# An FFT-filter and GELU-MLP kernel: the order of the first loads, the slots of batch 1's transform, and the slots of GpSimd's tables

## The chip, the cores and the metric

One core of one Trainium2 chip. The metric is the device time of one execution, in microseconds. The kernel takes x and the weights in float32 and gives float32; inside it works in bf16 and fp16.

Times in the text are microseconds from the start of the profiled span. A "slot" is one step of the main loop, defined below.

## The reference

```python
# x: (8, 3008, 256); filt_r, filt_i: (1505, 256); w_in: (256, 2048); w_out: (2048, 256)
X = np.fft.rfft(x, axis=1)
Y = X * (filt_r + 1j * filt_i)[None]
y = np.fft.irfft(Y, n=3008, axis=1).reshape(24064, 256)
h = y @ w_in
g = 0.5 * h * (1 + erf(h / sqrt(2)))
out = g @ w_out
```

So each of 8 batches goes through a global filter along its 3008 rows, and all 24064 rows go through a two-layer MLP with an exact GELU.

## The kernel before

**The transform.** The Fourier transform of length 3008 = 47 x 64 is done as small matmuls in four steps, s1 to s4. s1 is a transform over 47 rows; its result goes to DRAM (R1, stores on SP's queue) and comes back with other rows on the partitions (r1, tile b_sb). s2 is the transform over 64 with the twiddles; VectorE multiplies its result by the filters (s2_out, four products per unit) and adds the pairs (s2_sum, two pairs per unit). s3 is the first step back; ScalarE evicts it (s3_out), it goes to DRAM (R2) and comes back (r2, tile d_sb). s4 gives y, in a ring in SBUF. s1 works in four pieces c = 0 to 3 of the batch's input, s2 and s3 in three units u = 0 to 2, s4 in eight groups of two halves. Ahead of s1, fold takes sum and difference of the two halves of the input rows, on VectorE. Batch 0 has its own, quicker path (c1 to c4), which runs before the main loop.

**The MLP.** The rows are taken in 47 tiles of 512. mm1 makes 128 hidden columns of a tile (two matmuls of 512 columns, then a GELU on ScalarE); a tile takes 16 of them. mm2 multiplies by w_out. Tiles 0 and 2 do it plainly (mm2_first, 64 matmuls of 256 columns); all others with seven products in place of eight (mm2_seven, 112 matmuls of 128 columns), for which VectorE makes sums and differences of the hidden values (sums_1, four per tile; sums_2 and sums_3, two each) and of w_out (weight_sums, once).

**The main loop** counts slots s. Slot s does, in this order: what was put at s in a table written by hand (fold, s1, r1, s2, ..., tables), the share of the last tile's mm2, and one mm1 of tile s // 16. Every engine runs its instructions in the order in which this loop writes them. The mm2 of tile 0 begins at slot 10, four matmuls a slot to slot 15, and 8 for each 3 slots after that. Tile 5 is the first that needs batch 1's y: in its first six slots (80 to 85) no mm1 is done, and s4 of batch 1 begins at slot 82.

**Banks.** PSUM has three pools in the loop: "h" with 3 banks (mm1; one is lent to s1 with c > 1, to s2 and to s3), "o" with 2 banks (mm2; one is lent to s1 of batch 1 with c < 2, line 428), and "f" with 3 banks (s1 to s4, tables). An s1 takes four banks: VectorE evicts two of them, the lent one first, ScalarE the two others (lines 435 to 438).

**GpSimd.** GpSimd issues the loads that change the type (x, w_in, w_out; load_x_pairs and load_w_out), the later stores of the output (put_rows), and makes the tables: T1g and T2g (table_4_rows), wt (weights_4), pick (table_u_pick), T2p (table_2_parities), and T4a in four parts of eight columns w each (table_4_all, lines 406 to 416: two fp32 products and a sum, twice). It also loads half the rearranged filters (load_filters_again). s2 needs T2p and the filters, s3 needs U (table_u: two matmuls with pick), s4 needs T4a, each part for two groups. gate(t) (line 143) copies one element of t on GpSimd, so that what follows in GpSimd's queue starts only when t has been written.

**The first loads.** Ahead of the loop GpSimd issues batch 1's input, c = 0 then c = 2 (each call brings two pieces: c and c + 1), 12 transfers in all, and then the two halves of w_out:

```python
897    for c in (0, 2):
898        for h in range(2):
899            m.load_x_pairs(1, c, h, 2)
900    m.load_w_out(0)
901    m.load_w_out(8)
```

**Places of batch 1 before.** fold at slots 0, 1, 5, 8; s1 at 4, 7, 10, 12; r1 at 16; s2 at 30, 43, 56; s3 11 slots after each s2, at 41, 54, 67; r2 of piece 0 at 71. T1g, T2g, wt, pick and T2p are put at slot 0, table_4_factors at 14, table_u at 18, T4a's parts at 15, 45, 52 and 104.

Of the kernel before, what the change touches and what calls it, by code (L numbers as in the profile page):

```python
# [31 lines left out]
class _Mix:  # L32
# [385 lines left out]
    def s1(self, b, c):  # L418

        nc = self.nc  # L420
        if c == 0:
            self.st[b, "R1"] = self.dram.tile([NB, 48, 256], BF16, tag="R1", name="R1")
        if b == 1 and c == 3:
            at = self.pp.tile([128, 2, 4, 256], BF16, tag="p12", name="p12").rearrange("p t k c -> p (t k) c")
        else:
            at = self.pa.tile([128, 8, 256], BF16, tag="a", name="a_sb")
        x = self.st[b, "s", c], self.st["x1"][:, 1, 4 * c:4 * c + 4]
        lent = "o" if b == 1 and c < 2 else "h"
        ps = [[self.bank("ps_s1", lent if i == v == 0 else "f") for v in range(2)] for i in range(2)]
        for i in range(2):  # L430
            for d in range(2):
                for v in range(2):
                    nc.tensor.matmul(ps[i][v][64 * d:64 * d + 64, :], lhsT=self.T1s[64 * v:64 * v + NA],  # L433
                                     rhs=x[d][64 * v:64 * v + NA, 2 * i:2 * i + 2, :], start=True, stop=True)
        for i in range(2):
            for v in range(2):
                w = 4 * v + 2 * i
                self._evac(at[:, w:w + 2, :].rearrange("p w c -> p (w c)"), ps[i][v], "act" if v else False)
        for d in range(2):
            for v in range(2):  # L440
                w = HB * d + 16 * v + 4 * c
                nc.sync.dma_start(out=self.st[b, "R1"].rearrange("n q c -> q n c")[:, w:w + 4],
                                  in_=at[64 * d:64 * d + 48, 4 * v:4 * v + 4])
# [344 lines left out]
def kernel(  # L788
# [9 lines left out]
    m = _Mix(ctx, tc, x, filt_r, filt_i, moe_w_in, moe_w_out, out)  # L798
    nc, B, S = tc.nc, m.B, m.S
# [3 lines left out]
    g = m.small  # L803
    wide = ctx.enter_context(ExitStack())
    m.psum(wide, w=(2, 1), m=(1, 1), n=(5, 1))
    act = "act"
# [90 lines left out]
    for c in (0, 2):  # L897
        for h in range(2):
            m.load_x_pairs(1, c, h, 2)
    m.load_w_out(0)  # L900
    m.load_w_out(8)

    warm = g.tile([128, 1], FP32, name="warm")
    nc.scalar.activation(out=warm, in_=m.p, func=AF.Gelu)
# [9 lines left out]
    at = {}  # L914

    def put(slot, f, *a):
        at.setdefault(slot, []).append((f, a))

    def first(b):
        return (b * S // TCH) * 16  # L920

    busy, crowd, after = set(), set(), {}
    for b in range(1, B):
        hi = first(b)
        e = 4 * (b == B - 1)
        s1, n1, r1 = (4, 2.75, 16) if b == 1 else (hi - 87, 3.7, hi - 73) if b == 2 else (hi - 94 - e, 3.7, hi - 80 - e)
        s2 = (30, 43, 56) if b == 1 else (hi - 74, hi - 59, hi - 44) if e else (hi - 64 + (b == 2), hi - 48, hi - 32)
        busy.update(range(s1 - 1, s1 + int(3 * n1) + 2))
        for c in range(4):
            slot = s1 + int(c * n1 + (b == 1 and c in (1, 2)))  # L930
            put((0, 1, 5, 8)[c] if b == 1 else (70, 74, 86, 94)[c] if b == 2 else hi - 94 - (20, 13, 8, 6)[c], m.fold, b, c)
            put(slot, m.s1, b, c)
        for u in range(3):
            put(r1 if u < 2 else s2[0] + 1, m.r1, b, u)
            put(s2[u], m.s2, b, u)
            for i in range(4):
                put(s2[u] + 2 * i + (b == 2 and u == 0), m.s2_out, b, u, i // 2, i % 2)
            for i in range(2):
                put(s2[u] + (9 + i if 1 < b < B - 1 else 7 + 2 * i), m.s2_sum, b, 2 * u + i)
            s3 = s2[u] + (11 if b == 1 else 12 if e or (b, u) in ((2, 0), (B - 2, 2)) else 13)  # L940
            put(s3, m.s3, b, u)
            put(s3 + 1, m.s3_out, b, u, 1)
            busy.update(range(s2[u] - 1, s2[u] + 5), range(s3 - 1, s3 + 2))
        after[b] = s3 + 4
        crowd.update(range(s2[0], after[b]), range(s1 + 66, s1 + 94))
        if b + 1 < B:
            for i, (u, o, p) in enumerate(((0, 5, 1), (0, 7, 1), (1, 1, 2), (1, 5, 3), (1, 7, 3), (2, 1, 4), (2, 5, 5), (2, 7, 5))):
                put((76, 77, 80, 81)[i - 4] if b == 1 and i > 3 else s2[u] + o, m.load_next, b, p, i // 2, i % 2)

    for b in range(1, B):  # L950
        end = 1000000
        if b == B - 1:
            s4 = first(b) - 17
            for u in range(16):
                put(s4 + u, m.s4, b, u // 2, u % 2, act if u % 2 else False)
            for c in range(4):
                put(after[b] if c < 3 else s4 + 5, m.r2, b, c)
            continue
        for u in range(7, -1, -1):
            due = (b * S + GRP * u) // TCH * 16  # L960
            end = min(end, due - 2 if u or b > 1 else 83)
            if b == u == 1:
                end = 85
            for half in (1, 0):
                while end in busy:
                    end -= 1
                assert end > after[b] + 7
                put(end, m.s4, b, u, half, act if half or end in crowd or b == 1 and u == 0 else False)
                busy.add(end)
                end -= 1 if u < 3 else 2  # L970
            if u % 2 == 0:
                put(after[b] if u == 0 else end - 11, m.r2, b, u // 2)

    put(0, m.table_4_rows, g)
    put(0, m.weights_4, g)
    put(0, m.table_u_pick, g)
    put(0, m.table_2_parities)
    put(14, m.table_4_factors, g)
    put(18, m.table_u)
    parts = [(w, h) for w in range(0, HB, 8) for h in range(2)]  # L980
    for i, slot in enumerate((15, 45, 52, 104)):
        put(slot, m.table_4_all, parts[2 * i:2 * i + 2])
    put(1, m.load_filters_again, nc.gpsimd, 0, 2)
    put(18, m.load_filters_again, nc.sync, 2, 4)
    put(20, m.weight_sums)
    plain = (0, 2)
# [55 lines left out]
```

## Time and profile before

| | us |
|---|---|
| median of 3 runs | 737.6 (737.28 to 738.28) |
| the profiled execution, time | 737.13 |
| its span | 735.3 |
| first GELU of the main loop | 38.9 |
| ScalarE: 752 GELUs of 0.603 | 445.7 busy |
| VectorE: 84 filter products of 1.217 | 101.9 busy |
| GpSimd: issue of output stores | 131.7 busy |

The span is shorter than the device time by what lies around it, 1.8 us here. Busy TensorE counts pipelined matmuls with modelled ends, so a short stand between two matmuls hardly shows in the total: it is seen in the timeline of TensorE, where an instruction's idle time ahead of it and what released it stand in brackets. DVE is VectorE, ACT ScalarE, POOL GpSimd, SP the engine that issues most transfers between SBUF and DRAM.

In this execution the granted TensorE clock is 1.00 in all stretches of the span.

### The profile page before, as it was taken

The numbers are of one execution on the slowest core, as the hardware profiler recorded it, in microseconds if no ns is written. First come the engines' busy times: TensorE is split into PE (matmuls) and PEld (weight loads), VectorE is DVE, ScalarE is ACT, GpSimd is POOL, SyncE is SP. The second block draws the span as 40 slices with busy tenths as digits, with TensorE's granted clock in tenths as the row PEclk, the third lists the DMA queues.
The fourth block names the chain that finished last, engine by engine and source line by source line (L and its number), as shares of the span: only waits on it lengthen the run. The fifth ranks groups of instructions, "written<-read, shape, count | busy, mean of one in ns | idle before, by whom it ended". The sixth has DMA issues, their size and how long they took to land.

```text
span 735.3 us, 22145 instructions
## 1 busy us (share of the span) xinstructions
PE 716.1 (97%) x9063; PEld 506.5 (69%) x9213; DVE 604.6 (82%) x1105; ACT 575.4 (78%) x1049; POOL 291.2 (40%) x547
## 2 busy tenths in 40 slices
PE   8999999999999999999999999999999999999998
PEld 4856666677777767676677767666677767777776
DVE  8886797899887998789986989779998898675566
ACT  6997677688887888778887788877888788777773
POOL 7895744656122553134621355114631122122121
PEclk9999999999999999999999999999999999999999
DMA  8996435655345643545545455455544433311011
GB/s 145 211 187 213 107 91 116 196 144 110 83 132 172 125 99 105 149 145 117 119 124 171 104 115 124 116 151 132 120 109 127 148 100 102 111 38 52 30 58 59
DMA packets 81190, 89.30 MB, mean 121 GB/s; under 512 B 13201, under 2 KB 60433, under 8 KB 81089
## 3 DMA queue, kind: packets, MB, share of 16 engines
q0 software_dynamic: 22480, 40.02, 23.8%
q1 hardware_dynamic: 58193, 47.66, 23.4%
q8 instruction: 72, 1.18, 0.7%
q14 instruction: 29, 0.24, 0.1%
q10 hardware_dynamic: 416, 0.20, 0.1%
HBM read 55.57 MB, written 48.23 MB: 141 GB/s over the span
## 4 chain that ended last, share of the span: by engine, by line
PE 88%; DVE 3%; DMA 3%; POOL 2%; issue 2%; ACT 1%; DVEq 0%; POOLq 0%
PE ps_o L719 40%; PE ps_h L643 38%; PE ps_s L518 3%; DMA x_sb<-in_x_dram 2%; PE ps_o L659 2%; PE ps_s L433 2%; PE ps_s L491 2%; PE ps_s L460 2%; DMA F<-in_filt_i_dram 1%; ACT g_sb L646 1%; DVE g_sb L694 1%; POOL F L141 1%; DVE s_sb L688 1%; DVE a_sb L331 1%; POOL x_sb L90 0%
## 5 line engine op out<-in xcount | busy, mean ns | idle before, releaser
L646 ACT ACTIVATE g_sb<-ps_h 128x512 f16<-128x512 f32 x752 | 445.7, 603 | 138.8 <-PE ps_h L643 114.9
L643 PE MATMUL ps_h<-y_sb,w_in_sb 128*128 128x512 bf16 (+3 forms) x1454 | 414.2, 365 | 0.6
L766 POOL DMA_DIRECT2D out_dram<-ost x231 | 131.7, 577 | 380.5 <-DVE ost L748 370.0
L719 PEld LDWEIGHTS <-g_sb 128*128 128x128 f16 x2880 | 188.9, 98 | 84.4 <-issue 14.4
L719 PEld LDWEIGHTS <-s_sb 128*128 128x128 f16 x2160 | 145.3, 98 | 53.4 <-issue 3.1
L643 PEld LDWEIGHTS <-w_in_sb 128*128 128x128 bf16 x1600 | 125.7, 98 | 7.6 <-issue 1.3
L719 PE MATMUL ps_o<-w_sums,g_sb 128*128 128x128 f16 x1440 | 124.9, 219 | 2.4 <-DVE g_sb L694 0.9
L719 PE MATMUL ps_o<-w_sums,s_sb 128*128 128x128 f16 x1440 | 123.3, 219 | 1.9 <-DVE t_sb L734 0.2
L688 DVE TENSOR_TENSOR s_sb<-g_sb 128x1024 f16<-128x1024 f16 x180 | 119.2, 693 | 0.7 <-ACT g_sb L646 0.6
L719 PE MATMUL ps_o<-w_out_sb,g_sb 128*128 128x128 f16 x1440 | 116.4, 219 | 1.8
L471 DVE TENSOR_TENSOR p<-ps_s,F 128x1024 bf16<-128x1024 f32 x84 | 101.9, 1217 | 9.4 <-PE ps_s L460 8.0
L99 POOL DMA_DIRECT2D x_sb<-in_x_dram x156 | 79.4, 516 | 2.8 <-DMA x_sb<-in_x_dram 1.0
L694 DVE TENSOR_TENSOR g_sb<-s_sb,g_sb 128x1024 f16<-128x1024 f16 x90 | 63.7, 708 | 1.5
L719 PE MATMUL ps_o<-w_out_sb,s_sb 128*128 128x128 f16 x720 | 62.5, 219 | 0.9
L701 DVE TENSOR_TENSOR s_sb<-g_sb 128x1024 f16<-128x1024 f16 x90 | 61.5, 684 | 0.0
L741 DVE TENSOR_TENSOR t_sb<-t_sb,ps_o 128x256 f32<-128x256 f32 x45 | 18.8, 417 | 39.8 <-PE ps_o L719 39.3
L518 PEld LDWEIGHTS <-d_sb 96*128 96x128 bf16 x448 | 31.3, 97 | 26.0 <-issue 1.3
L329 ACT ACTIVATE y_sb<-ps_s 128x376 bf16<-128x376 f32 x95 | 45.5, 479 | 3.1 <-PE ps_s L518 3.1
L329 ACT ACTIVATE v_sb<-ps_s 128x512 bf16<-128x512 f32 x83 | 45.5, 608 | 1.5 <-PE ps_s L491 1.3
L748 DVE TENSOR_TENSOR ost<-t_sb,ps_o 128x256 f32<-128x256 f32 x88 | 32.9, 415 | 13.9 <-PE ps_o L719 13.8
L331 DVE CAST a_sb<-ps_s 128x512 bf16<-128x512 f32 x54 | 34.7, 684 | 11.6 <-PE ps_s L433 11.4
L736 DVE TENSOR_TENSOR ost<-t_sb,ps_o 128x256 f32<-128x256 f32 x45 | 18.6, 414 | 25.8 <-PE ps_o L719 25.8
(157 smaller groups left out, 563.5 us busy)
## 6 DMA issues: line engine op xcount, KB each, us to landing
out_dram<-ost POOLq DMA_DIRECT2D x127, 128.0 KB, 2.7
b_sb<-R SPq DMA_DIRECT2D x21, 512.0 KB, 4.6
R<-v_sb SPq DMA_DIRECT2D x84, 128.0 KB, 2.4
d_sb<-R SPq DMA_DIRECT2D x56, 192.0 KB, 4.1
R<-a_sb SPq DMA_DIRECT2D x108, 96.0 KB, 2.2
x_sb<-in_x_dram POOLq DMA_DIRECT2D x48, 94.0 KB, 2.8
x_sb<-in_x_dram POOLq DMA_DIRECT2D x48, 48.0 KB, 2.7
x_sb<-in_x_dram POOLq DMA_DIRECT2D x12, 188.0 KB, 5.3
```

Of the source, the lines that this page charges most:

```text
L99: self.nc.gpsimd.dma_start(out=xt[64 * v + to:64 * v + to + m, h, 4 * c:4 * c + 4 * n, :], in_=xv[h][at:at + m, w:w + 4 * n, :])
L329: self.nc.scalar.activation(out=out, in_=in_, func=AF.Copy, scale=1.0 if scale is None else scale)
L331: self.nc.vector.tensor_copy(out=out, in_=in_)
L471: v(out=w[:, a], in0=ps.unsqueeze(2).to_broadcast([128, 2, 2, 256]), in1=f.unsqueeze(1).to_broadcast([128, 2, 2, 256]), op=ALU.mult)
L518: nc.tensor.matmul(ps[:, 94 * i:94 * i + 94], lhsT=d[:, (grp % 2) * 4 + i, 128 * half:128 * half + 128], rhs=self.T4a[:, 4 * grp + i, 0:2 ...
L643: nc.tensor.matmul(ps[:, o:o + n], lhsT=w[:, dc], rhs=self.ring[:, dc, off:off + n], start=(dc == 0), stop=(dc == 1))
L646: nc.scalar.activation(out=self.st["g", t][:, jc, :], in_=ps, func=AF.Gelu)
L688: self.nc.vector.tensor_tensor(out=self.st["s", t][:, i:i + 2], in0=a, in1=b, op=ALU.subtract)
L694: self.nc.vector.tensor_tensor(out=a21[:, k], in0=self.st["s", t][:, k, 0], in1=a22[:, k], op=ALU.add)
L701: self.nc.vector.tensor_tensor(out=self.st["s4", t][:, k], in0=a12[:, k], in1=s2[:, k], op=ALU.subtract)
L719: nc.tensor.matmul(ps[:, (m + 1) % 2, sub, :], lhsT=a[:, i, 128 * sub:128 * sub + 128], rhs=b[:, i], start=i == 0, stop=i == 7)
L766: eng.dma_start(out=out, in_=tile_[lo - r0:lo - r0 + n])
```

## The change

Three things are changed, all near the start of the main loop. The first half of w_out is loaded between the two halves of batch 1's input. Batch 1's transform is put at other slots: s1 at 4, 8, 12, 14, fold at 0, 1, 7, 10, r1 at 18, s2 at 31, 45, 59, and so s3 at 42, 56, 70 and r2 of piece 0 at 74 (s4 stays at 82). GpSimd's tables move: a gate on what fold(1, 3) writes is put at slot 11, and T2p, the filters, pick, T1g, T2g and wt follow it; table_u goes from slot 18 to 24, table_4_factors from 14 to 38; T4a's parts go to 47, 54, 101 and 114, with a gate at 101 on the last a tile of batch 2's s1. In the changed kernel the lines from 427 up to the first loads have a number larger by one.

```diff
--- before.py
+++ after.py
@@ -424,6 +424,7 @@
             at = self.pp.tile([128, 2, 4, 256], BF16, tag="p12", name="p12").rearrange("p t k c -> p (t k) c")
         else:
             at = self.pa.tile([128, 8, 256], BF16, tag="a", name="a_sb")
+        self.st[b, "a"] = at
         x = self.st[b, "s", c], self.st["x1"][:, 1, 4 * c:4 * c + 4]
         lent = "o" if b == 1 and c < 2 else "h"
         ps = [[self.bank("ps_s1", lent if i == v == 0 else "f") for v in range(2)] for i in range(2)]
@@ -897,8 +898,7 @@
     for c in (0, 2):
         for h in range(2):
             m.load_x_pairs(1, c, h, 2)
-    m.load_w_out(0)
-    m.load_w_out(8)
+        m.load_w_out(4 * c)
 
     warm = g.tile([128, 1], FP32, name="warm")
     nc.scalar.activation(out=warm, in_=m.p, func=AF.Gelu)
@@ -923,12 +923,12 @@
     for b in range(1, B):
         hi = first(b)
         e = 4 * (b == B - 1)
-        s1, n1, r1 = (4, 2.75, 16) if b == 1 else (hi - 87, 3.7, hi - 73) if b == 2 else (hi - 94 - e, 3.7, hi - 80 - e)
-        s2 = (30, 43, 56) if b == 1 else (hi - 74, hi - 59, hi - 44) if e else (hi - 64 + (b == 2), hi - 48, hi - 32)
+        s1, n1, r1 = (4, 3.4, 18) if b == 1 else (hi - 87, 3.7, hi - 73) if b == 2 else (hi - 94 - e, 3.7, hi - 80 - e)
+        s2 = (31, 45, 59) if b == 1 else (hi - 74, hi - 59, hi - 44) if e else (hi - 64 + (b == 2), hi - 48, hi - 32)
         busy.update(range(s1 - 1, s1 + int(3 * n1) + 2))
         for c in range(4):
-            slot = s1 + int(c * n1 + (b == 1 and c in (1, 2)))
-            put((0, 1, 5, 8)[c] if b == 1 else (70, 74, 86, 94)[c] if b == 2 else hi - 94 - (20, 13, 8, 6)[c], m.fold, b, c)
+            slot = (4, 8, 12, 14)[c] if b == 1 else s1 + int(c * n1)
+            put((0, 1, 7, 10)[c] if b == 1 else (70, 74, 86, 94)[c] if b == 2 else hi - 94 - (20, 13, 8, 6)[c], m.fold, b, c)
             put(slot, m.s1, b, c)
         for u in range(3):
             put(r1 if u < 2 else s2[0] + 1, m.r1, b, u)
@@ -965,22 +965,24 @@
                 while end in busy:
                     end -= 1
                 assert end > after[b] + 7
-                put(end, m.s4, b, u, half, act if half or end in crowd or b == 1 and u == 0 else False)
+                put(end, m.s4, b, u, half, act if half or end in crowd or b == 1 and u < 2 else False)
                 busy.add(end)
                 end -= 1 if u < 3 else 2
             if u % 2 == 0:
                 put(after[b] if u == 0 else end - 11, m.r2, b, u // 2)
 
-    put(0, m.table_4_rows, g)
-    put(0, m.weights_4, g)
-    put(0, m.table_u_pick, g)
-    put(0, m.table_2_parities)
-    put(14, m.table_4_factors, g)
-    put(18, m.table_u)
+    put(11, lambda: m.gate(m.st["x1"][0:1, 1, 15, 0:1]))
+    put(11, m.table_2_parities)
+    put(11, m.load_filters_again, nc.gpsimd, 0, 2)
+    put(11, m.table_u_pick, g)
+    put(11, m.table_4_rows, g)
+    put(11, m.weights_4, g)
+    put(24, m.table_u)
+    put(38, m.table_4_factors, g)
+    put(101, lambda: m.gate(m.st[2, "a"][0:1, 3, 0:1]))
     parts = [(w, h) for w in range(0, HB, 8) for h in range(2)]
-    for i, slot in enumerate((15, 45, 52, 104)):
+    for i, slot in enumerate((47, 54, 101, 114)):
         put(slot, m.table_4_all, parts[2 * i:2 * i + 2])
-    put(1, m.load_filters_again, nc.gpsimd, 0, 2)
     put(18, m.load_filters_again, nc.sync, 2, 4)
     put(20, m.weight_sums)
     plain = (0, 2)
```

## The prediction

> **What bounds the kernel now.** I read the page's busy shares and its chain first, then busy time by stretch, then the timelines of TensorE, VectorE, GpSimd where the stretches show a hole.
>
> ```profile
> PE 716.1 (97%) x9063; PEld 506.5 (69%) x9213; DVE 604.6 (82%) x1105; ACT 575.4 (78%) x1049; POOL 291.2 (40%) x547
> PE 88%; DVE 3%; DMA 3%; POOL 2%; issue 2%; ACT 1%; DVEq 0%; POOLq 0%
> ```
>
> TensorE is busy 97% of the span and holds 88% of the chain. All matmul work stays after the change, so time moves only by the microseconds in which TensorE stands. Busy time by stretch (us; then PE, PEld, DVE, ACT, POOL) shows where it stands now:
>
> ```profile
> 42.00:46.00 4.00, 3.23 (x24) 1.13 (x22) 3.55 (x7) 4.00 (x9) 3.50 (x15) 1.00 1.22 192
> 70.00:75.00 5.00, 3.87 (x64) 2.39 (x63) 4.74 (x10) 2.72 (x5) 3.39 (x8) 1.00 0.49 71
> 130.00:140.00 10.00, 9.17 (x102) 6.06 (x102) 8.26 (x14) 6.93 (x13) 7.55 (x8) 1.00 0.62 161
> ```
>
> At 42 ScalarE is full (one gelu per slot, plus the evictions of s1); at 70 VectorE is full; at 130 it is slowed. The stalls by name, from the timeline of TensorE:
>
> ```profile
> 73.89 0.65 PE L491 MATMUL ps_s<-p,U 32*64 32x256 bf16 x16 [0.87 <-DVE p L477]
> 77.17 0.41 PE L460 MATMUL ps_s<-b_sb,T2p 64*32 64x256 bf16 x15 [0.22 <-ACT v_sb L329]
> 133.34 0.51 PE L719 MATMUL ps_o<-w_sums,g_sb 128*128 128x128 f16 x6 [0.72 <-DVE g_sb L694]
> ```
>
> And what feeds them, from the timelines of VectorE and GpSimd:
>
> ```profile
> 37.95 1.54 POOL L164 DMA_DIRECT2D w_out_sb<-in_moe_w_out_dram  x2 [0.39 <-DMA x_sb<-in_x_dram]
> 43.27 0.69 DVE L107 TENSOR_TENSOR x_sb<-x_sb 111x1024 bf16<-111x1024 bf16 x1 [0.42 <-DVE a_sb L331]
> 44.60 1.28 DVE L331 CAST a_sb<-ps_s 128x512 bf16<-128x512 f32 x2
> 93.30 2.54 DVE L688 TENSOR_TENSOR s_sb<-g_sb 128x1024 f16<-128x1024 f16 x2
> 130.67 2.62 DVE L694 TENSOR_TENSOR g_sb<-s_sb,g_sb 128x1024 f16<-128x1024 f16 x1
> 131.11 1.61 POOL L414 TENSOR_TENSOR tmp_sb<-t_sb 96x376 f32<-96x376 f32 x2
> ```
>
> The fold at 43.27 is put down to a cast that ended at 42.85; what it truly waits for is the last piece of batch 1's input, whose landing the trace records at 43.09. The two halves of w_out land next, at 46.02 and 49.14: GpSimd's queue lands strictly in order of issue and is never empty from 31 to 49 us. And an f16 add on VectorE, 0.68 alone, took 2.62 and 1.27 while GpSimd's fp32 products (L414, L416) ran.
>
> **The change, part by part** (like for like: TensorE's delay with the same work done).
>
> *A. w_out's first half ahead of input c=2, s1 at slots 4, 8, 12, 14.* The bytes up to and with the input's end are then those that before ended with w_out's first half: the last input lands at 46.02, not 43.09 (+2.9). On VectorE fold(1,2) stands at slot 7, ahead of the casts of s1(1) at slot 8, so these wait too: the first ends 2.15 after the landing (45.24 − 43.09 before), at 48.2. Behind it is TensorE: for c<2 s1 borrows an "o" bank, and the second matmul of mm2 at slot 10 needs that bank. TensorE gets there at about 44.4 (before, gelus 4 to 6 start at 41.82 to 42.78; one s1 less is ahead) and stands until 48.25, 3.8 us. From there: 3 mm2 0.33, mm1 0.43, slot 11 0.87, s1(2) 0.56 (119.36 to 119.92), slots 12 and 13 1.75, s1(3) 0.56: slot 14 at 52.75. Before, slot 14 with all four s1 done began at 50.64. **+2.1**; bounds 1.6 and 2.6, for a landing half a microsecond off. If the input were not delayed, the same count from 45.3 gives 49.8, −0.85.
>
> The longest stand of TensorE now, once the loop runs, is the 0.87 above, and the granted clock is 1.00 in every stretch, so no row prices what 3.8 us of idleness do to the clock; I take nothing for it. The Trainium skill (TensorE: Matmul & The Clock Gate, Part 1) says that an idle window of about 3.4 us halves the clock until about as long a busy one has passed. By that rule a drop would, as an estimate, add 1.7 us to the sum, and this wait would be long enough only by a little.
>
> *B. GpSimd's tables after a gate on fold(1,3).* Before, they filled 39.5 to 54 beside the folds. Now the gate opens 4.12 after the landing (47.21 − 43.09), at 50.1. Behind it in GpSimd's queue: gate 0.4, the T2p copies (eight; 0.49 alone, 5.6 in all as they ran), four F loads 2.25, pick (1.7 from its undisturbed rows, 2.5 as it ran): ready at 58.4 to 60.9. table_u on TensorE moves to slot 24, reached at 52.75 + 7.2 (gelu 14 at 52.00 to gelu 24 at 59.43, less table_u's own 0.24) = 59.95. I take **0**, since VectorE's sums now end before pick begins; bound +0.9. T1g, T2g and the weights (39.54 to 45.73 before) end by 67, ahead of table_4_factors at slot 38. The second w_out half is needed at slot 14, lands at 49. On SP, the last s1 stores go out 2.9 later, so b_sb lands near 62.4, and s2(0) at slot 31 starts near 65.3: hidden, with 2.9 to spare.
>
> *C. s2(0) at 31, s3(0) at 42.* VectorE's queue from s2 to the last sum: four products 1.13, two subtractions and two additions of tile 1 2.5, t 0.35, two L701 1.2, four sums 1.36, L736 and L739 0.78: 10.1, against 10.8 measured before (63.38 to 74.18; the copy of ost, 0.6, now comes ahead of s2). TensorE's own work up to s3 is 9.0 with the factors (0.3), now inside it; 8.6 before. Idle 0.85 in place of 1.7: **−0.85** (0 to −1.2).
>
> *D. s2(1) two slots after s3_out(1), not one.* ScalarE's four v evictions end 2.5 after s3; TensorE now comes 3 × 0.82 = 2.5 after it. The 1.28 that s2(1) took (76.23 to 77.51) falls to 0.6: **−0.65** (0 to −0.7).
>
> *E. T4a's last two parts.* The part that ran at 131 is now gated on the last s1 of batch 2, behind the L694 that it slowed: the 0.72 and its tail go, **−0.8** (0 to −0.9). The other (*G*) moves to slot 114, into s2(2,0), where one or two L701 (0.68) may become 1.3; s3 there has 0.7 of slack: **+0.4** (0 to 1.0).
>
> *F. s2(2) at slot 59, s3(2) at 70.* At 56 its four products came before three of tile 3's subtractions and one addition, and the sums ended at 100.03, 10.1 after 89.9, with TensorE waiting 0.2. Three slots later, all four subtractions, both additions and t stand ahead of the last sum: +0.6 + 0.6 + 0.35. T4a's second part (slot 54, behind load_next) again starts at the foot of this chain, so as at 93.30 two or three f16 operations lose 0.6 each. 8.9 + 1.55 + 1.2 = 11.7, while TensorE's way is 9.4 as before: idle near 1.8 in place of 0.2, **+1.6**. Bounds +0.9 (no overlap) and +2.5 (one add waits like the 2.62).
>
> *H. r2 at 74, s4 still at 82.* d landed 9.07 after s3(2) (100.41 to 109.48); TensorE now gets to s4 9.8 after it (ten slots of 0.82, two of 0.78) instead of 12.26. **0**, bound +0.5.
>
> Sum: 2.1 + 0 − 0.85 − 0.65 − 0.8 + 0.4 + 1.6 + 0 = **+1.8**. On the profiled execution (span 735.3, time 737.13) this is 738.9; the median of the runs is 0.5 above that execution, so **739.4** on it.
>
> **Rivals.** (1) *The input is not held back.* If the 16 DMA engines brought input and weights at the same time, A is −0.85 and the sum −1.15: 736.4, faster. It decides at a landing before about 44. For it: the change gives mm2 its weights 5 us earlier. Against: every landing on this queue from 31 to 49 came in order of issue. (2) *VectorE's new crowding in unit 2 stays hidden*, F 0.1: +0.3, 737.9. For it: TensorE comes later, VectorE does not, and it had slack at 86 (1.84 idle). Against: s2(0) now has the same mix and stood 0.87. (3) *Everything at its upper bound*: A 2.6, B 0.9, F 2.5, G 1.0, H 0.5 with the gains as taken: +5.2, 742.8; for it, B, F and G share the contention seen at 93.30 and 130.67. (4) *The gains do not come* (C, D, E at 0): +4.1, 741.7: against it, each wait has a named cause that moves away.
>
> **Numbers.** Forecast 0.45 (own range 738.2 to 740.8), rival 1 0.16, rival 2 0.19, rivals 3 and 4 0.10 each. About 0.2%, 1.5 us, is what can be told from no change: faster means below 736.1, slower above 739.1. Faster: two thirds of rival 1, some of rival 2: 0.17. Same: the rest of these and a quarter of the forecast: 0.28. Slower 0.55. Range 736.2 to 742.2, which leaves out the far halves of rivals 1 and 3.
>
> **What would show it.** A: fold(1,2) near 46.2 and an mm2 matmul of slot 10 waiting for a cast, till 48.2. B: table_u with no wait for pick. C, D: the waits of 73.89 and 77.17 halved and gone. F: s3(2) waiting over 1 us for L478. E: no wait like that of 133.34. The forecast is wrong if TensorE has no hole above 2 us between 44 and 49, or if unit 2 shows none.

## The result, and the profile after

| | before | after |
|---|---|---|
| median of 6 runs each, us | 737.69 (736.55 to 738.28) | 741.01 (739.49 to 743.22) |
| ratio to before, 95% interval | | 1.0047 [1.0029, 1.0066] |
| the profiled execution: time, span | 737.13, 735.3 | 743.22, 741.4 |

The change makes the kernel slower by 0.47%, some 3.3 us. The profiled execution of the changed kernel is the slowest of its six. It lies 6.1 us over the profiled one of before, which is more than the usual loss: its first GELU alone came 1.12 us later, and two of the places below (A and H) cost more in it than in other executions of the same code.

The page of the changed kernel, busy time and chain:

```profile
PE 718.0 (97%) x9065; PEld 506.7 (68%) x9213; DVE 603.1 (81%) x1105; ACT 575.8 (78%) x1049; POOL 286.6 (39%) x549
PE 80%; POOL 6%; issue 6%; DMA 3%; DVE 3%; ACT 1%; SPq 0%; DVEq 0%; POOLq 0%
```

TensorE's work is the same but for 1.9 us of busy time; its share of the chain fell from 88 to 80%. So the loss is mostly waits. A view that answers "where" at once is the list of all 752 GELUs of the main loop: the start of the n-th in one trace minus the start of the n-th in the trace of before is the delay built up so far (worked out from the timelines of ScalarE). The GELUs are counted from 0, so that up to number 79 the number is that of the slot. For the changed kernel the delay is +1.12 at the first GELU, +5.69 at number 40, +3.91 at 64, +5.77 at 74, +6.88 at 100, +5.99 at 104, and the same to the end. Everything happened in the first 135 us, in five places. The letters are those of the prediction's parts.

**At slot 10 (A).** The timelines of VectorE and TensorE (start, duration, instruction; in brackets the idle time before it and what ended that):

```profile
48.08 0.69 DVE L107 TENSOR_TENSOR x_sb<-x_sb 111x1024 bf16<-111x1024 bf16 x1 [3.71 <-DMA x_sb<-in_x_dram]
48.81 0.69 DVE L108 TENSOR_TENSOR x_sb<-x_sb 111x1024 bf16<-111x1024 bf16 x1
49.42 1.28 DVE L331 CAST a_sb<-ps_s 128x512 bf16<-128x512 f32 x2
```

```profile
45.80 0.27 PE L660 MATMUL ps_o<-w_out_sb,g_sb 128*128 128x256 f16 x1
50.15 0.49 PE L660 MATMUL ps_o<-w_out_sb,g_sb 128*128 128x256 f16 x3 [4.08 <-DVE a_sb L331]
52.51 1.07 PE L434 MATMUL ps_s<-x_sb,T1s 47*64 47x512 bf16 x8
```

fold(1, 2) waits 3.71 us for the input; the casts of s1(1) stand behind it; the second mm2 matmul of slot 10 needs their bank and TensorE stands 4.08 us. In the trace of before the four mm2 matmuls of slot 10 run without a stand:

```profile
46.28 0.61 PE L659 MATMUL ps_o<-w_out_sb,g_sb 128*128 128x256 f16 x4
```

The last line of the changed kernel shows a second thing: eight matmuls of s1 take 1.07 where they take 0.63 elsewhere. Busy time in stretches of 3.41 us (stretch; length; PE, PEld, DVE, ACT, POOL busy; then the granted clock, DMA share, GB/s) has the reason:

```profile
44.32:47.73 3.41, 1.75 (x14) 0.68 (x14) 0.05 (x1) 2.90 (x6) 0.00 (x0) 1.00 1.13 208
47.73:51.14 3.41, 0.99 (x8) 0.69 (x8) 3.02 (x5) 0.03 (x1) 0.00 (x0) 1.00 0.47 113
51.14:54.56 3.42, 3.42 (x19) 1.33 (x17) 2.13 (x4) 2.25 (x4) 2.39 (x6) 0.50 0.38 103
54.56:57.97 3.41, 3.36 (x27) 1.85 (x27) 1.67 (x3) 2.61 (x5) 3.37 (x8) 1.00 0.64 173
```

After a stretch in which TensorE was busy for 0.99 of 3.41 us, the clock is 0.50 for exactly the next one. TensorE is "busy" for all of it, and its matmuls take nearly twice as long (1.07 against 0.63 above).

**Units 0 and 1 (C, D).** In the changed kernel s3(0) and s2(1) each run as one row without a bracket, so neither stands longer than 0.15 at a time; before, s3(0) stood 0.87 and s2(1) 0.22. The delay falls by 1.77 between GELUs 40 and 64.

```profile
79.10 1.09 PE L492 MATMUL ps_s<-p,U 32*64 32x256 bf16 x32
82.70 0.63 PE L461 MATMUL ps_s<-b_sb,T2p 64*32 64x256 bf16 x32
```

**Unit 2 (F).** VectorE, GpSimd and TensorE:

```profile
98.35 1.22 DVE L472 TENSOR_TENSOR p<-ps_s,F 128x1024 bf16<-128x1024 f32 x1
99.48 1.24 DVE L689 TENSOR_TENSOR s_sb<-g_sb 128x1024 f16<-128x1024 f16 x1
100.64 1.21 DVE L472 TENSOR_TENSOR p<-ps_s,F 128x1024 bf16<-128x1024 f32 x1
101.78 1.24 DVE L689 TENSOR_TENSOR s_sb<-g_sb 128x1024 f16<-128x1024 f16 x1
```

```profile
96.23 1.63 POOL L414 TENSOR_TENSOR tmp_sb<-t_sb 96x376 f32<-96x376 f32 x2
97.93 1.34 POOL L416 TENSOR_TENSOR T4a<-tmp_sb 96x376 bf16<-96x376 f32 x1
99.35 2.06 POOL L414 TENSOR_TENSOR tmp_sb<-t_sb 96x376 f32<-96x376 f32 x2
101.49 0.98 POOL L416 TENSOR_TENSOR T4a<-tmp_sb 96x376 bf16<-96x376 f32 x1
```

```profile
103.67 0.44 PE L720 MATMUL ps_o<-w_out_sb,g_sb 128*128 128x128 f16 x5 [0.77 <-DVE ost L664]
106.73 0.51 PE L720 MATMUL ps_o<-w_sums,g_sb 128*128 128x128 f16 x6 [0.49 <-DVE g_sb L695]
```

Two of the differences take 1.24 in place of 0.68 while the products run (GpSimd's own instructions are lengthened in the same stretch, 1.34 and 2.06 in place of 0.98 and 1.6), and the queue behind them, the copy of tile 2's output (L664) and the sums, is late for TensorE.

**Behind r2 (H)**, GpSimd, then VectorE, then TensorE:

```profile
118.09 0.35 POOL L146 COPY gate<-d_sb 1x1 bf16<-1x1 bf16 x1 [12.12 <-DMA d_sb<-R]
...
121.81 2.35 POOL L767 DMA_DIRECT2D out_dram<-ost  x4
```

```profile
125.73 0.42 DVE L743 TENSOR_TENSOR ost<-t_sb,ps_o 128x256 f32<-128x256 f32 x1 [2.47 <-DMA out_dram<-ost]
126.06 0.41 DVE L746 TENSOR_TENSOR t_sb<-t_sb,ps_o 128x256 f32<-128x256 f32 x1
126.40 0.69 DVE L107 TENSOR_TENSOR x_sb<-x_sb 111x1024 bf16<-111x1024 bf16 x1
...
128.33 1.28 DVE L331 CAST a_sb<-ps_s 128x512 bf16<-128x512 f32 x2
```

```profile
129.06 0.59 PE L644 MATMUL ps_h<-y_sb,w_in_sb 128*128 128x512 bf16 x2 [0.52 <-DVE a_sb L331]
```

load_next's gate on d holds GpSimd's queue till 118.09. Tile 3's stores stand behind it and go out from 121.81; VectorE waits 2.47 for the ost buffer that they read; fold(2, 2) and the casts of s1(2, 0) come after, and TensorE waits for a cast. In the trace of before the gate opened at 108.75, 9.3 us earlier, while the loop here is only 5.8 us behind, and TensorE had no stand.

```profile
108.75 0.47 POOL L146 COPY gate<-d_sb 1x1 bf16<-1x1 bf16 x1 [7.86 <-DMA d_sb<-R]
```

**T4a's last parts (E).** The stand of 0.72, at 133.34 in the trace of before, is gone: −0.90.

### The profile page after: what moved, and what is told of

It reads as the page before. It is cut to its first block, busy times and chain, and to the rows that moved or that the text cites. A ratio compares the mean times of both kernels' runs of the same rounds, so it can differ in the third digit from the quotient of the medians.

```text
span 741.4 us, 22142 instructions
## 1 busy us (share of the span) xinstructions
PE 718.0 (97%) x9065; PEld 506.7 (68%) x9213; DVE 603.1 (81%) x1105; ACT 575.8 (78%) x1049; POOL 286.6 (39%) x549
## 4 chain that ended last, share of the span: by engine, by line
PE 80%; POOL 6%; issue 6%; DMA 3%; DVE 3%; ACT 1%; SPq 0%; DVEq 0%; POOLq 0%
PE ps_o L720 37%; PE ps_h L644 34%; PE ps_s L519 3%; DMA x_sb<-in_x_dram 2%; PE ps_s L434 2%; POOL x_sb L99 1%; PE ps_s L492 1%; PE ps_s L461 1%; POOL out_dram L767 1%; POOL tmp_sb L414 1%; ACT g_sb L647 1%; DMA F<-in_filt_i_dram 1%; POOL T4a L416 1%; PE ps_c L591 1%; POOL x_sb L90 1%
## 5 line engine op out<-in xcount | busy, mean ns | idle before, releaser
L689 DVE TENSOR_TENSOR s_sb<-g_sb 128x1024 f16<-128x1024 f16 x180 | 118.5, 689 | 0.7 <-ACT g_sb L647 0.6
L472 DVE TENSOR_TENSOR p<-ps_s,F 128x1024 bf16<-128x1024 f32 x84 | 101.9, 1217 | 8.1 <-PE ps_s L461 6.5
L695 DVE TENSOR_TENSOR g_sb<-s_sb,g_sb 128x1024 f16<-128x1024 f16 x90 | 61.8, 687 | 1.5
```

Source lines behind the costliest of these rows:

```text
L472: v(out=w[:, a], in0=ps.unsqueeze(2).to_broadcast([128, 2, 2, 256]), in1=f.unsqueeze(1).to_broadcast([128, 2, 2, 256]), op=ALU.mult)
L689: self.nc.vector.tensor_tensor(out=self.st["s", t][:, i:i + 2], in0=a, in1=b, op=ALU.subtract)
L695: self.nc.vector.tensor_tensor(out=a21[:, k], in0=self.st["s", t][:, k, 0], in1=a22[:, k], op=ALU.add)
```

## The experiments

Twelve kernels ran, four at a time on one chip, with the kernel before beside them (medians 737.27, 737.39 and 737.08 in the three groups); the row of the changed kernel is from its own six runs, beside a median of 737.69 for the kernel before. So ratios compare better than medians across groups. The table has the medians; to its right the delay against before's trace gained in each part of the loop, worked out as above from one profiled execution each.

| kernel | median, us | ratio to before | first GELU | A, to 40 | C+D, to 64 | F, to 74 | H, to 100 | E, to 104 | later |
|---|---|---|---|---|---|---|---|---|---|
| changed kernel | 741.01 | 1.0047 [1.0029, 1.0066] | 1.12 | 4.57 | −1.77 | 1.85 | 1.12 | −0.90 | 0.01 |
| e1_load_order | 736.48 | 0.9988 [0.9977, 0.9998] | 0.41 | 1.02 | −1.76 | 1.88 | 0.51 | −0.90 | 0.01 |
| e2_order_alone | 742.31 | 1.0059 [1.0045, 1.0072] | −0.05 | 5.62 | 0.00 | 0.01 | 0.00 | 0.00 | 0.01 |
| e3_casts_first | 736.91 | 0.9990 [0.9981, 0.9998] | −0.19 | 0.06 | −1.77 | 1.88 | 0.58 | −0.90 | 0.01 |
| e4_filler | 738.81 | 1.0019 [1.0010, 1.0027] | −0.21 | 2.21 | −1.77 | 1.88 | 0.44 | −0.90 | 0.21 |
| e5_units_back | 739.88 | 1.0032 [1.0019, 1.0046] | 0.61 | 4.17 | −0.03 | −0.21 | 0.00 | −0.90 | 0.01 |
| e6_t4a_later | 744.93 | 1.0103 [1.009, 1.0116] | 0.20 | 3.23 | −1.76 | 7.21 | 0.44 | −0.90 | 0.01 |
| e7_stores_on_sp | 743.12 | 1.0088 [1.0073, 1.0104] | 0.10 | 2.26 | −1.76 | 1.85 | 2.15 | −0.90 | 0.01 |
| e8_best_try | 736.77 | 0.999 [0.9982, 0.9999] | −0.32 | −0.01 | −0.85 | 0.40 | 0.76 | −0.90 | 0.01 |
| e9_t4a_gated | 737.55 | 1.0006 [0.9998, 1.0015] | 0.49 | −0.23 | −1.76 | 0.74 | 2.36 | −0.90 | 0.01 |
| e10_fold_behind | 737.24 | 1.0009 [0.9998, 1.002] | −0.02 | −0.16 | −1.77 | 1.88 | 1.33 | −0.85 | 0.97 |
| e11_both | 737.96 | 1.0017 [1.0005, 1.0029] | −0.23 | −0.25 | −1.76 | 0.74 | 3.76 | −0.85 | 1.31 |
| e12_best_second | 736.89 | 0.9995 [0.9986, 1.0004] | −0.60 | 0.45 | −0.85 | 0.41 | 0.25 | −0.84 | 1.28 |

How to read it: the columns C+D, F and E repeat to 0.03 us wherever the code of that part is the same, so they can be told to a tenth from one trace. The column "first GELU" is what the work ahead of the loop took in that execution, and A carries what DMA and clock did in that one execution.

### The loads: e1 to e4

e1, the changed kernel with only the loads put back:

```diff
             m.load_x_pairs(1, c, h, 2)
-        m.load_w_out(4 * c)
+    m.load_w_out(0)
+    m.load_w_out(8)
```

> The changed kernel with both halves of w_out loaded behind all of batch 1's input again; slots and GpSimd's order as changed. My theory (the loss is the wait of slot 10's second mm2 matmul for an o bank, behind a fold that waits for the late input, and the halved clock after it): the hole of 4.1 us goes, granted clock 1.00, about 737.3 (741.0 less 2.1 for the wait, 1.4 for the clock in most executions, 0.2 more at most). Rival (the later slots of s1 and of the units make the loss): it stays at 740 to 741.

Measured 736.48, ratio 0.9988. The hole is gone; what stands there instead is 0.99 us for w_out itself.

e2, the other way round, the kernel before with nothing changed but that order:

```diff
-    m.load_w_out(0)
-    m.load_w_out(8)
+        m.load_w_out(4 * c)
```

> The kernel before with the load order alone: w_out's first half between the halves of batch 1's input. My theory: s1(2) at slot 10 waits for the casts of s1(1) behind the fold, until about 5.7 us after what it does now less the landing's 2.9, so +3.1 and 1.7 more for a halved clock: 740.8 to 742.5. Rival (the slots make the loss): under 738.5.

Measured 742.31, ratio 1.0059. The pair settles it: by the ratios the order of the loads costs 0.59% in the changed kernel (1.0047 against 0.9988) and 0.59% alone, 4.4 us each time, and the rest of the change, taken by itself, is a gain of about 0.1%. That the two figures agree to the digit is partly chance: in e2's trace the half clock lasts two stretches, 6.8 us in place of 3.4, and e1 pays the 0.99 for w_out.

e3, the changed kernel with the order of the loads kept and fold(1, 2) behind the casts of s1(1):

```diff
-            put((0, 1, 7, 10)[c] if b == 1 ...
+            put((0, 1, 9, 10)[c] if b == 1 ...
```

> The changed kernel with fold(1, 2) at slot 9, so that VectorE does the casts of s1(1) ahead of the fold that waits for the input. My theory: mm2 at slot 10 finds its o bank free, TensorE stands only at slot 12, about 1.2 us, clock 1.00: 737.6 (741.0 less 2.0 and less 1.4). Rival 1 (TensorE waits for the input itself, wherever the fold stands): the hole moves to slot 12 and keeps 3 us or more, 740 to 741. Rival 2 (the slots): 741.

Measured 736.91. VectorE:

```profile
44.15 1.29 DVE L331 CAST a_sb<-ps_s 128x512 bf16<-128x512 f32 x2 [0.50 <-PE ps_s L434]
46.12 0.69 DVE L107 TENSOR_TENSOR x_sb<-x_sb 111x1024 bf16<-111x1024 bf16 x1 [0.69 <-DVE a_sb L331]
```

The casts end at 45.4 and TensorE doesn't miss the bank. The fold starts 2.9 us later than in the kernel before (46.12 against 43.27), for an input that stands where the change put it, and that costs nothing. So it isn't the late input as such that made the hole: it is a late input with the casts of another piece queued behind it on VectorE.

e4 fills the hole, with 14 matmuls on constants into a free bank, which add to no output:

```diff
+    def keep_busy(n):
+        ps = m.bank("ps_warm", "f")
+        for i in range(n):
+            nc.tensor.matmul(ps, lhsT=m.ones[:, 0:128], rhs=m.ones, start=True, stop=True)
+
+    put(10, keep_busy, 14)
```

> The changed kernel with 14 matmuls of 512 columns on constants (about 3.0 us, their result is not used) at slot 10, inside the hole. My theory: the wait itself stays and TensorE goes on at the same moment, but the granted clock stays 1.00 and the 1.7 us of half clock go: 739.5, and less spread. Rival (the clock record is not what lengthens slots 10 to 13): 741, or later by what the filler overhangs.

Measured 738.81: 2.2 us less (2.1 by the ratios) for 3.2 us of added work. The added matmuls run inside the wait, 0.47 of which is left; the clock is 1.00 throughout, and A is 2.21.

### The units, the products and the stores: e5 to e8

e5: `s2 = (31, 43, 56) if b == 1` in place of `(31, 45, 59)`.

> The changed kernel with the units of batch 1's transform at slots 31, 43 and 56 in place of 31, 45 and 59 (s3 at 42, 54, 67, r2 of piece 0 at 71); the order of the loads, s1's slots and the tables stay as changed. Theory: the later slots cost 1.9 us at unit 2 (TensorE standing at 103.67, 106.73 and 108) and 1.1 us behind r2 (VectorE's 2.47 at L743), and gave 0.65 at s2(1), which comes back as a wait. So 741.0 - 1.9 - 1.1 + 0.65 = 738.7, no TensorE stand over 0.5 us between 96 and 110 and none at the folds of batch 2, but one at s2(1). Rival 1, unit 2's wait is T4a's contention alone and moves with the unit: 740.6. Rival 2, all that the change lost is at the loads (A), and the slots cost nothing: 741.7.

Measured 739.88, 1.2 above the expectation. In the trace F and H go to −0.21 and 0.00, as expected; but all of C + D goes too, 1.74, where 0.65 was counted. The gain of C is there (the delay falls by 1.47 from GELU 40 to 42) and is given back two slots later, where s2(1), now one slot after s3_out(1), waits for ScalarE (TensorE):

```profile
81.42 0.27 PE L461 MATMUL ps_s<-b_sb,T2p 64*32 64x256 bf16 x1 [0.57 <-ACT v_sb L329]
81.91 0.41 PE L461 MATMUL ps_s<-b_sb,T2p 64*32 64x256 bf16 x15 [0.22 <-ACT v_sb L329]
```

With 1.85 + 1.12 + 0.21 won and 1.74 lost, 1.4 should be left, and the medians differ by 1.1.

e6, T4a's second part at slot 72: `enumerate((47, 72, 101, 114))`.

> The changed kernel with T4a's second part at slot 72 in place of 54, where GpSimd stood idle for 12.12 us; all else as changed. Theory: of the 1.9 us at unit 2, 1.2 is VectorE's f16 operations losing 0.6 each beside GpSimd's products, and 0.7 the longer queue on VectorE; the first part goes: 739.8, with L689 at 0.68 each around 99 to 102 and the stand at 103.67 gone, one of about 0.5 left at s3(2). Rival, the longer queue alone makes the wait: 741.0 and the same stands. Rival 2, the products slow VectorE just as much at their new place, beside batch 1's last sums: the stand moves to about 108 to 114, 741.0 or above.

Measured 744.93, against all three. A slot only says what stands ahead of an instruction in its queue. GpSimd had nothing else, so the products ran from 102.3, as soon as a store had gone, while TensorE came to s3(2), put at slot 70, only at 106.87; and now they ran beside VectorE's very last sums (VectorE, then TensorE):

```profile
101.90 2.57 DVE L689 TENSOR_TENSOR s_sb<-g_sb 128x1024 f16<-128x1024 f16 x1
104.51 1.35 DVE L695 TENSOR_TENSOR g_sb<-s_sb,g_sb 128x1024 f16<-128x1024 f16 x1
```

```profile
105.91 0.51 PE L720 MATMUL ps_o<-w_sums,g_sb 128*128 128x128 f16 x6 [2.85 <-DVE g_sb L695]
```

TensorE stood 2.85 us, and then for 6.8 us its clock was 0.50. The part itself was wrongly placed, and the run says nothing on how unit 2's price divides; e9 mends that.

e7, tile 3's stores on SP's queue:

```diff
-                                      nc.gpsimd if t > 1 or h * sub == 0 else nc.sync)
+                                      nc.gpsimd if t > 1 and t != 3 or h * sub == 0 and t != 3 else nc.sync)
```

> The changed kernel with the stores of tile 3's output on SP's queue, not on GpSimd's, so that they don't stand behind the gates on d. Theory: the 2.47 that VectorE waited at L743 for out_dram, and with it the late fold of batch 2 and TensorE's stands at 127 and 129, come from the stores' place behind the gate: the wait goes, 0.5 to 1.1 us less, 739.9 to 740.5. Rival, the ost buffers come free late for another reason (the DMA engines are full there), or the late d itself holds TensorE: the wait at L743 stays over 1 us, 741.0.

Measured 743.12. The wait at L743 is gone, as the theory said, and the time isn't. VectorE:

```profile
119.99 0.42 DVE L743 TENSOR_TENSOR ost<-t_sb,ps_o 128x256 f32<-128x256 f32 x1
120.32 0.42 DVE L746 TENSOR_TENSOR t_sb<-t_sb,ps_o 128x256 f32<-128x256 f32 x1
123.13 0.69 DVE L107 TENSOR_TENSOR x_sb<-x_sb 111x1024 bf16<-111x1024 bf16 x1 [2.40 <-DMA x_sb<-in_x_dram]
```

The fold starts 8.2 us after the gate (114.96), and in the changed kernel it started 8.3 after it (126.40 − 118.09), but not for the same reason. There the last piece of its input had landed at 124.50, 6.4 after the gate, and the fold stood behind L743; here that piece lands at 122.84, 7.9 after the gate, and the fold waits for it. So the new queue took one wait away, and the input, loaded behind the same gate on d, came later and made another. Why these loads took longer with the stores on SP's queue isn't shown, and the run doesn't say what the stores' wait alone costs. TensorE's one stand of 2.06 here is longer than the two that it replaces; why the median is also higher than the changed kernel's, by more than the 1.0 of column H, stays open.

e8 puts the casts first and the units at 31, 44, 57.

> The changed kernel with fold(1, 2) at slot 9, as in the run with the casts first (736.9), and with units at 31, 44 and 57: one slot later than before for s2(1) to clear s3_out(1), and unit 2 only one slot later than before. Theory: the gains at the tables and at s2(1) stay, unit 2's 1.9 falls to about 0.5 and the 0.5 behind r2 goes: 735.0. Rival, unit 2 stands as long as before, since T4a's part and the products move with it: 736.9.

Measured 736.77; in the trace F is 0.40 and C + D −0.85. It isn't told apart from e3 by the median.

### Unit 2 and the fold, one at a time: e9 to e12

e9 to e11 are built on e3, e12 on e8. e9 adds a gate, so that GpSimd's products can't start before s3_out(2); lines behind 498 have a number larger by one in it:

```diff
+        self.st[b, "v"] = vt
...
-    for i, slot in enumerate((47, 54, 101, 114)):
+    put(72, lambda: m.gate(m.st[1, "v"][0:1, 0, 0:1]))
+    for i, slot in enumerate((47, 72, 101, 114)):
```

> The kernel of the run with the casts first (736.9: the changed kernel with fold(1, 2) at slot 9), with T4a's second part put at slot 72 behind a gate on what s3_out(2) writes, so that GpSimd's products can't start beside unit 2. (In the run with the part at slot 72 and no gate they started as soon as GpSimd had nothing else, at 102.3, and slowed the sums that mm2 and s3 waited for.) Theory: unit 2's price is two parts, two f16 operations that lose 0.56 each beside the products, and VectorE's longer queue; the first part goes: 735.8, the stands between slots 68 and 70 falling from 2.6 to about 1.4. Rival, all of it is VectorE's queue: 736.9 and 2.6. Rival 2, the products now slow tile 3's sums around 108 and TensorE stands there: 736.9 or more, with L689 above 0.68 at 105 to 112.

Measured 737.55. Both the theory and the second rival hold. F falls from 1.88 to 0.74, by the 1.1 expected; and the products, now at 104.5 to 111.4, slow tile 3's sums (VectorE, then TensorE):

```profile
107.15 1.36 DVE L108 TENSOR_TENSOR x_sb<-x_sb 111x1024 bf16<-111x1024 bf16 x1
108.44 0.41 DVE L743 TENSOR_TENSOR t_sb<-t_sb,ps_o 128x256 f32<-128x256 f32 x1
...
109.55 2.98 DVE L690 TENSOR_TENSOR s_sb<-g_sb 128x1024 f16<-128x1024 f16 x3
```

```profile
113.24 0.84 PE L721 MATMUL ps_o<-w_out_sb,g_sb 128*128 128x128 f16 x12 [1.84 <-DVE ost L750]
```

The time that unit 2 gave back, 1.1, is paid at the next place, and more: H goes from 0.58 in e3 to 2.36.

e10 puts fold(2, 2) at slot 93, `(70, 74, 93, 94)[c] if b == 2`, behind the casts.

> The kernel of the run with the casts first (736.9), with batch 2's fold(2, 2) at slot 93 in place of 86, so that the casts of s1(2, 0) and s1(2, 1) at slots 89 and 92 no longer stand behind it on VectorE. Theory: what the change lost behind r2 is the same as at slot 10: a fold that waits for its input (its load stands behind the gate on d; it started 8.2 to 8.3 after the gate with the stores on either queue), ahead of casts that TensorE waits for. The stand at slots 86 to 88 goes: 0.5 less in this kernel, 736.4. Rival, VectorE is held by its output buffer at L743, not by the input, and the casts stay as late: 736.9.

Measured 737.24. The rival held: with the fold out of the way VectorE still waits 2.72 for out_dram at L743, and H is 1.33. In e3 that wait was 1.93, and the fold's input had landed at 118.39, 1.0 before L743 could go on (119.41): the stores, not the input, held the casts there. Both kernels issue the stores at the same moment (115.83 and 115.77), yet the wait is 0.8 longer here; why isn't known, so that H may have grown by that execution's transfers and not by the edit. No kernel with both waits taken away was tried. The fold, later by seven slots, also makes s1's stores late, and s2(2, 0) at 144.80 waits 0.54 for b_sb: the three kernels with the fold there have such a wait, e9 hasn't.

> The two edits together, gated products and the fold behind the casts: 736.9 - 1.1 - 0.5 = 735.3 if the two are independent waits; 735.8 or above if removing the one only moves the time to the other (TensorE arriving earlier at the later place).

Measured 737.96, above both expectations. H is 3.76, but the stands of e9 and e10 don't add up in it. TensorE has e9's stand (1.82 at 112.48, where e9 has 1.84 at 113.24) and one of 0.20, and none of e10's (0.94 at 122.17). The rest is a stretch of half clock from 114.3 to 117.7, which, as an estimate, costs half its 3.4 us, 1.7.

> The kernel with units at 31, 44, 57 and the casts first (736.8), with fold(2, 2) at slot 93. Theory: its stand of 0.84 at slot 86 to 88 goes: 736.1. Rival, the time moves on to the next wait: 736.8.

Measured 736.89, the same as e8: H falls from 0.76 to 0.25, and 1.28 comes back when s2(2, 0) waits 1.20 for b_sb. The fastest versions, e1, e3 and e8, are some 0.6% faster than the changed kernel by the ratios and 0.1% faster than the one before, which is hardly more than can be told.

## Why the prediction was right or wrong

The forecast of 739.4 had the sign, and 741.01 is inside its range; 1.6 us of the cost were not in the sum. The half clock, for which the sum has nothing, was worth about 2 (e4); the other misses have both signs and partly cancel, which is luck.

- **A, +2.1: the wait was right, the clock was left out.** Against the landing of c = 0 the input came 2.9 later, as the sum had it (47.81 − 40.01 in the changed kernel, 43.09 − 38.16 in the kernel before). With the clock at 1.00 the loss is 2.21 (e4) and 2.26 (e7's execution). In the executions with half clock it is 3.23, 4.17 and 4.57, which also differ in when their input landed; in the last TensorE's stand was 4.1, not 3.8. "I take nothing for it" is the step that failed. The Trainium skill (TensorE: Matmul & The Clock Gate, Part 1), which the prediction weighed, says that an idle window of about 3.4 us halves the clock until about as long a busy one has passed. The trace agrees in the length, 3.413 us at 0.50, but not in the idleness: TensorE was busy for 0.99 us of the stretch before. The prediction's estimate by that page, 1.7 us, is half of 3.413, and e4 without the half clock was faster by 2.2 us (2.1 by the ratios), so the size was right to about half a microsecond.
- **B, 0: right.** table_u didn't wait for pick, which was ready at 61.1; TensorE came to it at 63.90.
- **C and D, −0.85 and −0.65: together −1.77, so mis-sized by 0.3.** The split was off: C brings 1.47 and D the other 0.30, and e5 shows that without D the next wait takes nearly all of it back.
- **F, +1.6: measured 1.85.** e9 gives the parts: 1.1 for the two slowed differences (1.2 predicted) and 0.74 for the longer queue.
- **E, −0.8: −0.90.** **G, +0.4: nothing** could be seen at slot 114.
- **H, 0 with a bound of 0.5: wrong, 1.12** in the profiled execution and 0.44 to 0.58 in three others with the same code here (e1, e3, e4). e5, with the units back, has 0.00, so it comes from the later slots. The step asked only whether s4 would wait for d. It missed that load_next's gates on d stand in GpSimd's queue ahead of tile 3's stores, and that batch 2's next input is behind them as well. It followed what is queued behind the new gates and not what is queued behind the old gate whose opening moved. That the stores' wait at L743 is the link is read from the traces (in the changed kernel the input was there 1.2 before L743 could go on); no run with the units at these slots took that wait away without another stand in its place.
- **Rival 1** (the input isn't held back) fell with the landing at 47.81 and with e1 and e2. **Rival 2** (unit 2 hidden) fell with 1.85. **Rival 4** (741.7) was nearest in time, by chance: the gains, which it left out, came in full. **Rival 3** (742.8) lies about as far above as the forecast lies below, and by other terms: B and G cost nothing, A without the clock and F stayed below its bounds, and the clock, which it didn't have, cost about 2.
- The sum by the measured terms without the clock is 2.2 − 1.77 + 1.85 − 0.90 = +1.4, and H makes it +1.9 to +2.5. The one run of six whose clock was 1.00 took 739.49, that is 1.8 above the median of before and 2.4 above its profiled execution. The other five took 739.87 to 743.22. So the forecast's time nearly fits that one run, but with F and H too small by 0.7 to 1.4 in all, and C, D, E and G too dear by 0.8.

## What to carry to other kernels

When an input is made later, look at what stands behind its first user in that engine's queue: moving the user behind the casts (one number) was worth 4 us, as much as undoing the new order of the loads. A slot in the program orders a queue but starts nothing: where an engine runs ahead, only a gate keeps its work off a busy stretch, and then the next stretch has to bear it. When a step moves, every old wait on its result moves too, with all that is queued behind that wait.

## What the hardware showed

**The clock goes by fixed stretches.** All changes of the granted clock in a trace lie on a grid of 3.413 us, counted on from the change at the span's start. The changed kernel and e5 to e7 have nearly the same hole, but it falls differently on the grid. e5, with a shorter stand than the changed kernel's (2.78 us):

```profile
46.60:50.02 3.42, 0.78 (x6) 0.50 (x6) 2.81 (x5) 1.02 (x3) 0.00 (x0) 1.00 0.79 178
50.02:53.43 3.41, 3.41 (x19) 1.33 (x17) 1.94 (x4) 2.04 (x4) 2.17 (x6) 0.50 0.41 111
```

and e7, with a stand of 3.54 that two stretches share:

```profile
43.21:46.62 3.41, 1.65 (x14) 0.62 (x14) 0.29 (x1) 2.80 (x6) 0.00 (x0) 1.00 1.10 206
46.62:50.03 3.41, 1.62 (x11) 0.97 (x10) 3.34 (x6) 0.60 (x1) 0.00 (x0) 1.00 0.63 146
50.03:53.45 3.42, 3.37 (x32) 1.72 (x33) 2.01 (x4) 2.95 (x6) 2.99 (x8) 1.00 0.51 136
```

A stretch with TensorE busy 0.78 to 1.25 of 3.41 us was followed by 0.50 each time, in five cases (the changed kernel, e2, e5, e6 twice), and stretches with 1.62 to 1.75 by 1.00 in the changed kernel and e7; but e11 has one with 1.62 that was followed by 0.50, so the bound lies about there and isn't busy time alone. The stretch need not be wholly idle, and a stand that is longer can cost less. In e2, and in e6 the second time, the clock stayed at 0.50 for a second stretch: TensorE had been busy for 2.64 and 2.08 us of the first. Where it was busy for 3.06 us or more of a stretch at 0.50, the next one was at 1.00.

**Only some of VectorE's instructions are slowed beside GpSimd.** In e9's lines above L108, whose two inputs are in SBUF, takes 1.36 where it takes 0.69 alone, and L743, with one input in PSUM, its 0.41 as always; so do the products L472 (1.22, one input in PSUM) beside L689 (1.24 for 0.68) in the changed kernel. That agrees with the Trainium skill (SBUF — State Buffer, Who interferes with whom): a VectorE instruction with two SBUF inputs contends with a GpSimd instruction that reads SBUF. The runs don't separate the place of the operands from their type: those that are slowed are in 2-byte types, those that aren't read float32. By the page, which operations can share a stretch with GpSimd's products is to be read from their operands.
